# Padding the tiles that alpha, q and k are loaded into from 384 to 512 bytes per head

## The chip, the cores and the metric

The kernel runs on one core of one Trainium2 chip. The metric is the device time of one execution in microseconds (us). It is taken without the profiler; a further execution with the hardware profiler gives the profile. The engines are named as the profile names them: PE is TensorE (PEld its weight loads), DVE is VectorE, ACT is ScalarE, POOL is GpSimd and SP is SyncE, which here only issues transfers. DMA stands for the 16 engines that move data between DRAM and the on-chip memory SBUF.

## The reference

The first half is a recurrent linear attention with a decay for each key dimension; the second is a feed-forward layer whose hidden value is the largest of three products and zero.

```python
# q, k, v, alpha: (B, H, S, D) = (4, 8, 768, 48), float32; alpha in 0.8..1.0
for t in range(S):
    state = alpha[:, :, t, :, None] * state + np.einsum('bhd,bhe->bhde', k[:, :, t], v[:, :, t])
    y[:, :, t] = np.einsum('bhd,bhde->bhe', q[:, :, t], state)
x = y.transpose(0, 2, 1, 3).reshape(B * S, H * D)                 # 3072 x 384
h = np.maximum(np.maximum(x @ w1, x @ w2), x @ w3)                # w: 384 x 768
out = h @ w_out                                                   # 3072 x 384, float32
```

The feed-forward has no explicit rectifier in the reference. The kernel writes the largest of three as x @ w1 plus the larger of 0, x @ (w2 - w1) and x @ (w3 - w1); this is why it has a bypass product, w1 @ w_out, and differences of weights.

## The kernel before, in words

The sequence of 768 steps of each of the 4 batch entries is cut into 3 chunks of 256 steps, so there are 12 groups, numbered n = 4 * chunk + batch entry, and the four batch entries take turns. Within a group the 256 steps lie on 128 partitions, two neighbouring steps (r = 0, 1) on one partition. For each group there are four loads (`load`, L274), one each for alpha, q, k and v. A load brings, for each of 128 partitions and 8 heads, the two steps' 2 x 48 floats, which lie next to each other in DRAM: 384 bytes. For the first group each load is cut in two by heads, 4 heads each (HH). The destination tiles are in `ld`, named an, qn, kn and vn in the profile; each of them has NL = 5 buffers, so loads run up to five groups ahead of their use.

From alpha come the products of the two steps (`aa`, L351, on POOL or DVE), the logarithms (`la`, L356 and L361, on ACT), and by a matmul with a triangular matrix (L426) their sums along the chunk. The exponentials of these sums (ep and en, L435, on ACT) scale q and k (`qk`, L440, on POOL or DVE, 48 instructions in all, each for 4 heads). v is scaled and cast to half precision (L259 on ACT or L261 on POOL). Then come transposes (L465), the copy of the transposed q and k (L479), the scores within the chunk (L491), their masking (L499), the state (L523, L412, L400), and the output within the chunk (L578) and from the state (L556). The result is turned (L599) to xT, which the feed-forward reads.

The feed-forward of a group (`ffn`) is 36 products with the differences of weights (L622), their rectification and maximum (L631, L633, L638), the products with w_out and the bypass (L658, L655), a copy out of PSUM (L255) and a store of 192 KB (L674). It follows the attention of its group by about four groups. The weights come in four transfers from POOL's queue (`weights`, L288 and L291), 576 KB each as written; their differences are taken on DVE (L308).

All of this is cut into 821 steps, numbered as the code creates them. The order in which they are issued, and the engine and the PSUM banks of each, are written out by hand in the string `ORDER` (L26 to L70): `12A` is step 12 on ACT, `67G` step 67 on POOL. `Plan.emit` (L101) only checks that what a step reads has been issued before it. Each engine goes through its own instructions in that order and waits on semaphores for the others. All loads and stores are issued by SP in one queue; the weights are issued on POOL's queue among POOL's own work.

The tiles come from one pool and lie one behind the other in each partition, in the order in which they are created: constants first, then the 20 load tiles of `ld` (5 of alpha, 5 of q, 5 of k, 5 of v), and then all others.

Of the kernel before, what the change touches and what calls it, by code (L numbers as in the profile page):

```python
# [10 lines left out]
FP32 = mybir.dt.float32  # L11
# [103 lines left out]
def kernel(  # L115
# [14 lines left out]
    B, H, S, D = q.shape  # L130
# [3 lines left out]
    P = 128  # L134
# [43 lines left out]
    def homes(n, shape, dtype, name):  # L178
        return [sb.tile(shape, dtype, name=f"{name}{i}") for i in range(n)]

    NL, NQ, NT_, HH = 5, 6, 4, H // 2
    ld = {x: homes(NL, [P, H, 2, D], FP32, x + "n") for x in "aqkv"}
    aas = homes(2, [P, H, D], FP32, "aa")
    las = homes(3, [P, 2, H, DP], FP16, "la")
    eps = homes(3, [P, HH, 2, D], FP32, "ep")
# [545 lines left out]
```

## Time and profile before

| | us |
|---|---|
| median of 3 runs | 151.62 |
| lowest and highest run | 150.16, 151.63 |
| span of the profiled execution | 148.5 |
| PE busy in the span | 130.6 |
| DVE busy in the span | 121.9 |
| ACT busy in the span | 80.7 |
| POOL busy in the span | 71.8 |

The profiled execution's own time is its span, from the first instruction to the last; the times of the runs hold besides it what lies before and after. The page lists, for each group of instructions, its line and engine, what it writes and reads with partitions x elements and type, how many there are, their busy time, the mean duration in ns, and the idle time of the engine just before them with what ended it. The row of digits for DMA gives the busy share of the 16 DMA engines in 40 slices of 3.7 us each, in tenths. The chain is the work that ended last, followed backwards from the last instruction through what released each step.

The transfers of the page, by queue: q1 holds SP's loads and stores (53,584 packets, 23.60 MB, 63.4% of the 16 engines' time), q0 the weights that POOL issues (832 packets, 2.36 MB, 8.1%). DRAM was read at 23.63 MB and written at 4.72 MB.

### The profile page before, as it was taken

What the parts mean: (1) busy time and instruction counts of PE and PEld (TensorE: products, weight loads), DVE (VectorE), ACT (ScalarE), POOL (GpSimd) and SP (SyncE); (2) the same over time, 40 slices, a digit from 0 to 9 for tenths busy, and PEclk for the clock granted to TensorE, in tenths of its full rate; (3) what the DMA queues carried; (4) which work ended last, traced back from release to release, by engine and by line L of the source; (5) the groups of instructions that cost most, each with busy time, mean ns of one, the idle gap of its engine ahead of it and who ended that gap; (6) DMA issues with size and microseconds to landing.
All of it is one profiled execution on the core that took longest, in us unless ns stands there. A gap on an engine that the chain in (4) does not pass through costs nothing.

```text
span 148.5 us, 5617 instructions
## 1 busy us (share of the span) xinstructions
PE 130.6 (88%) x2389; PEld 101.7 (68%) x2389; DVE 121.9 (82%) x231; ACT 80.7 (54%) x182; POOL 71.8 (48%) x114
## 2 busy tenths in 40 slices
PE   0136588889999999999999999999999999999990
PEld 0025576767776678887687889777777788787670
DVE  6489996999899979998896899699698786789720
ACT  3665156796895987947877759328622820000011
POOL 8105810431859888999976678994720100000000
PEclk9999999999999999999999999999999999999999
DMA  4999999999999999999997299601211100031223
GB/s 111 257 261 262 258 214 212 279 231 265 270 262 265 261 275 267 262 288 268 233 279 188 79 246 280 200 3 60 106 57 57 53 4 0 4 119 40 85 99 134
DMA packets 54728, 26.34 MB, mean 177 GB/s; under 512 B 50736, under 2 KB 54320, under 8 KB 54704
## 3 DMA queue, kind: packets, MB, share of 16 engines
q1 hardware_dynamic: 53584, 23.60, 63.4%
q0 software_dynamic: 832, 2.36, 8.1%
q8 instruction: 18, 0.29, 0.9%
q10 hardware_dynamic: 288, 0.04, 0.3%
q14 instruction: 6, 0.05, 0.1%
HBM read 23.63 MB, written 4.72 MB: 191 GB/s over the span
## 4 chain that ended last, share of the span: by engine, by line
PE 65%; DMA 10%; POOL 6%; ACT 5%; DVE 4%; SPq 4%; issue 3%; POOLq 0%; DVEq 0%
PE psum L622 26%; PE psum L658 15%; PE psum L655 8%; DMA wcat<-in_moe_w_dram 6%; SPq L274 4%; DMA qn<-in_q_dram 4%; POOL qk L440 3%; PE psum L491 3%; PE psum L578 3%; PE psum L465 2%; PE psum L599 2%; PE psum L334 2%; PE psum L556 2%; PE psum L523 2%; POOL Z L400 1%
## 5 line engine op out<-in xcount | busy, mean ns | idle before, releaser
L622 PE MATMUL psum<-xT,d 128*128 128x256 f16 x432 | 54.1, 273 | 0.9 <-DVE d L308 0.5
L622 PEld LDWEIGHTS <-d 128*128 128x128 f16 x432 | 40.0, 98 | 7.0 <-DVE d L308 1.5
L499 DVE TENSOR_TENSOR LA<-psum,d 128x1024 f16<-128x1024 f32 x24 | 28.7, 1218 | 3.7 <-PE psum L491 2.8
L658 PE MATMUL psum<-wo,hT 128*128 128x384 f16 (+1 forms) x150 | 27.5, 320 | 0.0
L638 DVE TENSOR_TENSOR hT<-psum,hT 128x512 f16<-128x512 f32 x36 | 23.7, 681 | 2.9 <-PE psum L622 2.6
L440 POOL TENSOR_TENSOR qk<-qn,ep 128x384 f16<-128x384 f32 x18 | 18.3, 1026 | 11.3 <-DMA qn<-in_q_dram 9.2
L631 ACT ACTIVATE hT<-psum 128x512 f16<-128x512 f32 x28 | 16.4, 601 | 12.7 <-PE psum L622 12.3
L255 ACT COPY ob<-psum 128x384 f32<-128x384 f32 x14 | 6.7, 481 | 27.8 <-PE psum L658 27.8
L658 PEld LDWEIGHTS <-hT 128*128 128x128 f16 x150 | 14.5, 98 | 8.9
L440 POOL TENSOR_TENSOR qk<-kn,en 128x384 f16<-128x384 f32 x16 | 15.9, 999 | 9.0 <-ACT en L435 8.5
L479 DVE COPY qkT<-psum 128x1024 f16<-128x1024 f16 x24 | 16.0, 683 | 0.9 <-PE psum L465 0.7
L655 PE MATMUL psum<-past,xT 128*128 128x384 f16 (+1 forms) x75 | 15.8, 320 | 0.0
L259 ACT ACTIVATE xb<-psum,c 128x384 f16<-128x384 f32 x17 | 9.3, 583 | 9.0 <-PE psum L578 9.0
L435 ACT ACTIVATE en<-psum 128x384 f32<-128x384 f32 x24 | 11.5, 493 | 2.1 <-DVE psum L430 2.1
L465 PE MATMUL psum<-d,qk 64*128 64x64 f16 x384 | 8.8, 198 | 4.1 <-POOL qk L440 2.1
L435 ACT ACTIVATE ep<-psum 128x384 f32<-128x384 f32 x24 | 11.6, 493 | 1.1 <-DVE psum L430 0.8
L351 POOL TENSOR_TENSOR aa<-an 128x384 f32<-128x384 f32 x9 | 9.0, 1001 | 4.7 <-DVE qkT L479 4.2
L255 ACT CAST xT<-psum 128x384 f16<-128x384 f32 x20 | 9.4, 482 | 3.0 <-PE psum L599 2.8
L426 PE MATMUL psum<-la,c 128*128 128x192 f16 x24 | 6.1, 271 | 5.5 <-ACT la L361 5.5
L465 PEld LDWEIGHTS <-qk 64*128 64x128 f16 x384 | 7.0, 99 | 5.5 <-DVE qk L440 2.9
L400 POOL TENSOR_TENSOR Z<-U,G 48x192 f16<-48x192 f32 x10 | 5.0, 504 | 11.8 <-DVE U L412 11.5
L430 DVE TENSOR_TENSOR psum<-psum,la 128x192 f32<-128x192 f32 x24 | 8.5, 358 | 2.6 <-PE psum L426 1.8
(58 smaller groups left out, 196.4 us busy)
## 6 DMA issues: line engine op xcount, KB each, us to landing
out_dram<-ob SPq DMA_DIRECT2D x23, 192.0 KB, 2.0
an<-in_alpha_dram SPq DMA_DIRECT2D x11, 384.0 KB, 6.2
qn<-in_q_dram SPq DMA_DIRECT2D x11, 384.0 KB, 5.7
kn<-in_k_dram SPq DMA_DIRECT2D x11, 384.0 KB, 6.2
vn<-in_v_dram SPq DMA_DIRECT2D x11, 384.0 KB, 6.3
wcat<-in_moe_w_dram POOLq DMA_DIRECT2D x2, 576.0 KB, 10.3
w1s<-in_moe_w_dram POOLq DMA_DIRECT2D x1, 576.0 KB, 7.9
wo<-in_moe_w_out_dram POOLq DMA_DIRECT2D x1, 576.0 KB, 7.8
```

The costliest lines, as they stand in the source:

```text
L255: (nc.scalar.copy if eng == "ACT" else nc.vector.tensor_copy)(out=out, in_=in_)
L259: nc.scalar.activation(out=out, in_=in_, func=AFT.Copy, scale=factor)
L435: lambda eng, t=t, sign=sign: nc.scalar.activation(out=t, in_=live[Lk], func=AFT.Exp, scale=sign),
L440: lambda eng, w=w, x=x, e=e: on[eng].tensor_mul(qk[:, w, :, :, :D].rearrange("p r h d -> p h r d"), ld[x][n % NL][:, hs], e),
L465: nc.tensor.transpose(live["tp", v][:, i, at:at + HALF], qks[v % NQ][rows, w, r, 2 * j:2 * j + 2, :], ident[rows, rows])
L479: lambda eng: nc.vector.tensor_copy(out=qkT.rearrange("p i w j t -> p i (w j t)"), in_=live["tp", u]),
L499: lambda eng: nc.vector.tensor_mul(LA.rearrange("p a j r t -> p (a j) (r t)"), live[Ak].rearrange("p a (j t) -> p (a j) t", j=2), maskA.un ...
L622: nc.tensor.matmul(live[gk][:, jj, :], hidden(apart[g][j][:, kt], jj), xT[:, kt, :], start=(kt == 0), stop=(kt == NFT - 1))
L631: nc.scalar.activation(out=h, in_=live[gk], func=AFT.Relu)
L638: lambda eng, h=h, gk=gk: nc.vector.tensor_max(h, live[gk], h),
L655: nc.tensor.matmul(live[ok], xT[:, kt, i * P:(i + 1) * P], past[:, kt, cols], start=(kt == 0), stop=False)
L658: nc.tensor.matmul(live[ok], hT[:, kt, i * P:(i + 1) * P], wo16[:, kt, cols], start=False, stop=(kt == NJ - 1))
```

## The change

The tiles of alpha, q and k are created with 8 x 128 floats on each partition instead of 8 x 2 x 48. Of each head's 128 floats (512 bytes) the first 96 (384 bytes) are used, seen as 2 x 48 as before; the other 32 are neither written nor read. v's tiles keep 8 x 2 x 48 floats, back to back. All other code takes its views from these, so the loads write, and the engines read, the same elements at other places. Fifteen tiles grow from 3,072 to 4,096 bytes per partition.

```diff
     NL, NQ, NT_, HH = 5, 6, 4, H // 2
-    ld = {x: homes(NL, [P, H, 2, D], FP32, x + "n") for x in "aqkv"}
+    ld = {x: [t[:, :, :2 * D].rearrange("p h (r d) -> p h r d", r=2) for t in homes(NL, [P, H, 2 * D if x == "v" else P], FP32, x + "n")] for x in "aqkv"}
     aas = homes(2, [P, H, D], FP32, "aa")
```

## The prediction

> **What bounds the kernel now.** I read the page first: its busy shares, the rate of the transfers, and the costliest groups.
>
> ```profile
> span 148.5 us, 5617 instructions
> PE 130.6 (88%) x2389; PEld 101.7 (68%) x2389; DVE 121.9 (82%) x231; ACT 80.7 (54%) x182; POOL 71.8 (48%) x114
> DMA  4999999999999999999997299601211100031223
> DMA packets 54728, 26.34 MB, mean 177 GB/s; under 512 B 50736, under 2 KB 54320, under 8 KB 54704
> q1 hardware_dynamic: 53584, 23.60, 63.4%
> PE 65%; DMA 10%; POOL 6%; ACT 5%; DVE 4%; SPq 4%; issue 3%; POOLq 0%; DVEq 0%
> ```
>
> TensorE is the bound: it is busy for 88% of the span and holds 65% of the chain that ended last. The transfers are full for the first half of the span (the row of nines) and hold 10% of the chain. Nearly all packets are under 512 bytes: the 12 groups of four 384 KB loads make 12 x 4 x 1,024 = 49,152 packets of 384 bytes (one head, two rows of 48 floats). They are what the change touches.
>
> Next, the stages: columns are the stretch, its length, the busy time of PE, PEld, DVE, ACT and POOL, the granted clock, the share of the 16 DMA engines (over 1 when packets overlap) and the rate.
>
> ```profile
> core 0: us, PE busy (x) PEld busy (x) DVE busy (x) ACT busy (x) POOL busy (x), PEclk, DMA share, GB/s
> 0.00:5.00 5.00, 0.00 (x0) 0.10 (x1) 2.85 (x17) 1.60 (x2) 3.60 (x15) 1.00 0.59 134
> 5.00:10.00 5.00, 1.79 (x28) 0.90 (x27) 3.51 (x10) 4.33 (x13) 0.00 (x0) 1.00 1.20 272
> 10.00:15.00 5.00, 2.75 (x94) 2.14 (x88) 4.73 (x10) 2.14 (x5) 2.23 (x3) 1.00 1.27 263
> 15.00:20.00 5.00, 3.21 (x113) 2.78 (x117) 4.90 (x6) 0.95 (x2) 3.68 (x6) 1.00 1.19 244
> 20.00:25.00 5.00, 4.71 (x79) 3.88 (x79) 4.07 (x9) 3.17 (x9) 0.00 (x0) 1.00 1.06 215
> 25.00:30.00 5.00, 4.05 (x39) 3.23 (x38) 4.41 (x9) 3.80 (x9) 1.78 (x2) 1.00 1.14 261
> 30.00:35.00 5.00, 4.40 (x124) 3.44 (x123) 4.94 (x9) 4.76 (x10) 1.16 (x2) 1.00 1.15 254
> 35.00:40.00 5.00, 4.75 (x71) 3.52 (x68) 4.36 (x10) 3.26 (x8) 3.18 (x5) 1.00 1.04 256
> 45.00:50.00 5.00, 5.00 (x81) 3.21 (x80) 4.87 (x10) 3.33 (x10) 4.41 (x6) 1.00 1.22 264
> 75.00:80.00 5.00, 5.00 (x104) 3.77 (x103) 4.60 (x12) 4.01 (x11) 3.12 (x6) 1.00 1.05 284
> ```
>
> The reader is to see two regimes. Up to about 25 us TensorE is short of work; from 40 us it has no gap, so there a load may come earlier or later without moving the end, as long as it comes before its use. The granted clock is 1.00 throughout. The chain shows which transfers count in the first regime (start, length, what):
>
> ```profile
> 6.45 0.64 SPq L274
> 7.14 5.45 DMA qn<-in_q_dram
> 12.73 1.38 POOL qk L440
> 14.12 0.71 issue
> 14.83 0.80 POOL qk L440
> 15.77 9.15 DMA wcat<-in_moe_w_dram
> 25.42 0.56 DVE d L308
> 27.31 2.15 PE psum L622 x18
> ```
>
> The second group's q lands at 12.59 us, releases the multiply on POOL, and behind it on POOL's queue stand the weight loads, which land at 24.92 us and open the feed-forward part.
>
> **The change, part by part.** No instruction is added, removed or moved on any engine: the order is written out by hand and the dependencies are the same. Three things differ.
>
> *1. Where the loads write.* A load still writes 128 partitions x 8 heads x 384 bytes from the same addresses in DRAM, so 1,024 packets of 384 bytes. Before, the eight heads lay back to back (start every 384 bytes); now every 512, with a gap of 128. In the built program the first alpha tile starts at byte 17,856 of its partition in both kernels, which is 448 past a multiple of 512. Before, heads start at 448, 320, 192, 64 past such a multiple, in turn. Now all start at 448, since the new tiles are 4,096 bytes long. So 512 bytes per head do not bring alignment to 512: every head straddles such a boundary, where before three in four did. Counted in 256-byte blocks, a head touched 3 blocks (starts 448 and 192) or 2 (320 and 64), 2.5 in the mean; now always 3.
>
> What is a packet's time? At 263 to 284 GB/s over 16 engines, 16 x 384 bytes / rate gives 21.6 to 23.4 ns. All four starts are already in these rates, and nothing in the windows separates them. If the block count set the price, a, q and k would cost 20% more (3 against 2.5); if it plays no part, nothing. Below nothing: the best rate in the rows is 284 against 263 to 272 in the early stretch, so 4 to 8% could be won if the packing back to back were what holds the early packets up. I take nothing: the nearest rows are those of the loads themselves, in which every second head already starts as all will start now (192 past a 256-byte boundary). The ends +20% and -8% stay for the range.
>
> The Trainium skill ("DMA: Bandwidth & Descriptors", section "How a descriptor splits into AXI transactions") says that a descriptor is cut at 256-byte boundaries, and that one with an unaligned start also pays for the bytes before it. By that a write of 384 bytes starting 192 past a boundary is 18 beats and one starting 64 past it 14, so an estimate from that page is 16 in the mean before and 18 after, 12.5% more; the section's examples are reads, and no view of before shows what writes pay. This rule speaks against the change, and with it the slower rival below would cost +0.9 to +1.5 us in place of what is worked out there.
>
> *2. What the engines read.* Five kinds of instruction read the padded tiles. Alpha's readers (L351, L356) already step over half a head at a time: a step of 384 bytes becomes 512. The multiplies of L440 read one run of 384 floats before and four runs of 96 now.
>
> ```profile
> L440 POOL TENSOR_TENSOR qk<-kn,en 128x384 f16<-128x384 f32 x16 | 15.9, 999 | 9.0 <-ACT en L435 8.5 <-POOL Z L400 0.4
> L351 POOL TENSOR_TENSOR aa<-an 128x384 f32<-128x384 f32 x9 | 9.0, 1001 | 4.7 <-DVE qkT L479 4.2 <-DMA an<-in_alpha_dram 0.4
> 6.66 0.56 DVE L351 TENSOR_TENSOR aa<-an 128x384 f32<-128x384 f32 x1 [0.45 <-DMA an<-in_alpha_dram]
> 7.49 0.56 DVE L440 TENSOR_TENSOR qk<-kn,en 128x384 f16<-128x384 f32 x1
> L356 ACT ACTIVATE la<-an 128x384 f16<-128x384 f32 x11 | 5.9, 536 | 0.0
> L361 ACT ACTIVATE la<-aa 128x384 f16<-128x384 f32 x11 | 5.8, 526 | 1.0 <-POOL aa L351 0.8
> ```
>
> L351 reads both operands in runs of 48 with gaps, L440 one run; on POOL they take 1001 and 999 ns, on VectorE 0.56 and 0.56 us. On ScalarE, reading with gaps (L356) against without (L361) is 536 against 526 ns. So gaps cost at most 10 ns here. Upper bound: 10 ns x 48 multiplies = 0.5 us over two engines, little of it on the chain, where POOL has 6%. I take nothing.
>
> *3. Addresses and issue.* Fifteen tiles grow by 1,024 bytes, so what lies behind them moves by up to 15,360 bytes, a multiple of 512: their place in such blocks stays. The loads' issue on SP:
>
> ```profile
> 72.07 0.43 SPq L274 DMA_DIRECT2D qn<-in_q_dram  x1
> 75.83 0.38 SPq L274 DMA_DIRECT2D vn<-in_v_dram  x1
> L674 SPq DMA_DIRECT2D out_dram<-ob x25: 332/357/2130, 52.2 to 145.7; - x25
> ```
>
> An unblocked load of 1,024 packets is issued in 0.38 to 0.43 us, an output with 128 packets in 0.33 at least: the number of pieces hardly counts, and the early issues of about 1.4 us are the queue waiting for the engines. The form of the access (partition, head, 96 floats) is the same. Nothing again.
>
> Sum: 0. The span stays 148.5 us. The three runs' median, 151.62, stands 3.1 us above the span; that remainder lies outside what the profile shows, and I leave it. Forecast **151.6 us**. The runs shown spread from 150.16 to 151.63, about 1%, which is what a measurement of this kernel can tell from no change.
>
> **What a dearer or cheaper packet is worth.** Before q's second load lands at 12.59 us, SP has issued eight half loads and two whole ones: 8 x 192 + 2 x 384 KB = 2.36 MB, 8.9 us at 265 GB/s. Of these, v has 384 KB and a, q, k the other 83%. One per cent on their packets is 0.074 us there. Then the weights share the engines with queued loads:
>
> ```profile
> qn<-in_q_dram SPq DMA_DIRECT2D x11, 384.0 KB, 5.7
> wcat<-in_moe_w_dram POOLq DMA_DIRECT2D x2, 576.0 KB, 10.3
> ```
>
> From 12.6 to 25 us, 2.4 us x 263 + 5 x 244 + 5 x 215 GB/s = 2.9 MB go by; less two or three weight matrices of 0.59 MB, 1.2 to 1.75 MB are loads, 4.4 to 6.6 us at 265 GB/s: some 60% of 8.9 us again. After that the cover is the pace of the compute:
>
> ```profile
> L440 POOL TENSOR_TENSOR qk<-qn,ep x18: 992/1002/1379, 12.7 to 107.4; 128x384 f16<-128x384 f32 x18
> L440 DVE TENSOR_TENSOR qk<-qn,ep x6: 541/555/559, 8.9 to 88.8; 128x384 f16<-128x384 f32 x6
> ```
>
> The 24 multiplies of q run from 8.9 to 107.4 us: 4.3 us for each, 8.6 for a group, whose four loads are 1.57 MB or 5.9 us at 265 GB/s. The loads would have to be some 40% slower before they set the pace of the whole. If they did, the time would be far off, up in the 160s.
>
> **Rivals.** *Slower: each head's write pays for the third block.* Place: the loads before 25 us; price 20% on a, q, k. The first 8.9 us grow by 0.83 x 20% = 1.5 us, the weights come up to 0.9 us later still, so +1.5 to +2.4 and 153.1 to 154.0 us. TensorE's idle time between 25 and 40 us (0.95 + 0.60 + 0.25 = 1.8 us) may swallow some. It decides (over 1%) from about 15% more per packet. For it: the start of the span is bound by transfers and the change leaves only straddling starts. Against it: nothing in the rates shows two prices. A heavier form belongs here too: if the engine now joins the eight back-to-back writes of a partition into one run of 3,072 bytes, and the gaps stop it, the price could be higher than 20%. The packet count shows 384-byte pieces already, so I give it little. I name 153.4 us for this rival, and 0.30.
>
> *Faster: separate slots ease the early loads.* In the early stretch and at 45 us the packets overlap (share 1.20 to 1.27 at 263 to 272 GB/s), at 75 us they don't (1.05 at 284). If neighbouring heads in one 512-byte block hold each other up, the gap lets the early loads run at 284: 4 to 8% of 8.9 us, 0.4 to 0.6 us, and with the weights up to 0.9: 150.7 to 151.2. Over 1% it would need 15% faster packets, which no row shows. Against it: the same packing is there at 75 us, where the rate is full. I give 0.17 to a time over 1% below, mostly for what the rows can't show.
>
> *No effect, because the change doesn't reach what limits a packet*: it stays at 384 bytes, under 512 as before. This is the forecast, 150.2 to 152.6 by the runs' spread on either side, 0.53.
>
> **How the numbers follow.** 0.53 for the forecast, within 1% (150.1 to 153.1); 0.30 for slower by over 1%; 0.17 for faster. The range: 149.6 takes in the faster rival and 0.6 below it for an unshown gain, 154.4 the slower rival's upper end with as much again of the spread; below and above these I leave 0.08 and 0.12.
>
> **What would show it.** Right: q1's packets and share unchanged (53,584, 63.4%), 263 to 272 GB/s between 5 and 15 us, q's second load landing near 12.6 us, the weights near 25, L440 on POOL at 999 to 1026 ns. The slower rival: fewer GB/s before 15 us at the same packet count, and landings later by a tenth. The faster: over 280 GB/s there. Wrong in another way: L440 or L351 longer on POOL or VectorE, or a packet count that changes.

## The result and the profile after

The changed kernel takes 155.84 us in the median of its runs (155.64 to 157.21), the kernel before 150.89 us beside it. The ratio is 1.036, with a 95% interval of 1.029 to 1.042: the change costs 5 us. The forecast was no change, with a range up to 154.4; the slower rival gave 153.1 to 154.0 us. Each ratio, here and below, compares undisturbed runs with runs of the kernel before beside them on the same chip, while a median in us takes in all runs; so across chips the ratios are to be compared.

The page of the changed kernel, in the lines that answer to those shown of before:

```profile
span 154.0 us, 5617 instructions
PE 133.2 (86%) x2389; PEld 102.8 (67%) x2389; DVE 123.4 (80%) x231; ACT 81.1 (53%) x182; POOL 71.9 (47%) x114
q1 hardware_dynamic: 53584, 23.60, 71.4%
PE 36%; ACT 0%; issue 0%
```

The span is 5.5 us longer. The packets are the same in number and bytes, but their share of the engines' time is 71.4% of a longer span, where it was 63.4%: each packet is in flight longer. The chain can't be followed back beyond 95.7 us in this trace, so the stages have to show the rest (columns as in the prediction):

```profile
core 0: us, PE busy (x) PEld busy (x) DVE busy (x) ACT busy (x) POOL busy (x), PEclk, DMA share, GB/s
5.00:10.00 5.00, 1.33 (x12) 0.45 (x11) 3.15 (x8) 4.49 (x13) 0.00 (x0) 1.00 1.31 228
10.00:15.00 5.00, 3.25 (x104) 2.59 (x104) 4.17 (x11) 2.23 (x6) 0.97 (x1) 1.00 1.33 225
15.00:20.00 5.00, 2.31 (x76) 1.89 (x76) 4.93 (x6) 0.61 (x1) 3.91 (x7) 1.00 1.32 239
20.00:25.00 5.00, 4.34 (x98) 3.48 (x99) 4.79 (x10) 2.46 (x5) 1.00 (x1) 1.00 1.05 214
45.00:50.00 5.00, 5.00 (x107) 3.66 (x108) 4.56 (x11) 4.48 (x12) 3.34 (x6) 1.00 1.28 225
75.00:80.00 5.00, 4.77 (x66) 3.73 (x66) 4.28 (x9) 4.57 (x13) 4.10 (x5) 1.00 1.23 229
```

Wherever only loads run, 263 to 284 GB/s have become 225 to 229. Only from 15 to 25 us, where the weights run beside the loads, is the rate about as before (239 against 244, then 214 against 215). The instructions on POOL that read the padded tiles are no slower:

```profile
L351 POOL TENSOR_TENSOR aa<-an 128x384 f32<-128x384 f32 x9 | 9.0, 999 | 9.7 <-DVE LA L499 8.3 <-DMA an<-in_alpha_dram 1.2
L440 POOL TENSOR_TENSOR qk<-qn,ep 128x384 f16<-128x384 f32 x18 | 18.1, 1018 | 13.3 <-DMA qn<-in_q_dram 9.9 <-ACT ep L435 2.6 <-ACT xb L259 0.7
```

So what the change itself made dearer is the transfers. Two things that come of it show up only in single rows, and are taken up below: slower products on TensorE after 28 us, although the clock of the rows above is 1.00, and three longer instructions on VectorE near 90 us.

### The profile page after: what moved, and what is told of

Its sections match the earlier page's. It is cut to its first block, busy times and chain, and to the rows that moved or that the text cites. A ratio compares the mean times of both kernels' runs of the same rounds, so it can differ in the third digit from the quotient of the medians.

```text
span 154.0 us, 5617 instructions
## 1 busy us (share of the span) xinstructions
PE 133.2 (86%) x2389; PEld 102.8 (67%) x2389; DVE 123.4 (80%) x231; ACT 81.1 (53%) x182; POOL 71.9 (47%) x114
## 3 DMA queue, kind: packets, MB, share of 16 engines
q1 hardware_dynamic: 53584, 23.60, 71.4%
## 5 line engine op out<-in xcount | busy, mean ns | idle before, releaser
L622 PE MATMUL psum<-xT,d 128*128 128x256 f16 x432 | 55.7, 278 | 1.8 <-DVE d L308 1.8
L622 PEld LDWEIGHTS <-d 128*128 128x128 f16 x432 | 41.0, 100 | 8.4 <-DVE d L308 2.0
L499 DVE TENSOR_TENSOR LA<-psum,d 128x1024 f16<-128x1024 f32 x24 | 28.7, 1217 | 3.5 <-PE psum L491 2.6
L440 POOL TENSOR_TENSOR qk<-qn,ep 128x384 f16<-128x384 f32 x18 | 18.1, 1018 | 13.3 <-DMA qn<-in_q_dram 9.9
L440 POOL TENSOR_TENSOR qk<-kn,en 128x384 f16<-128x384 f32 x16 | 16.2, 1013 | 8.9 <-ACT en L435 7.8
L351 POOL TENSOR_TENSOR aa<-an 128x384 f32<-128x384 f32 x9 | 9.0, 999 | 9.7 <-DVE LA L499 8.3
L491 PE MATMUL psum<-qkT 48*64 48x128 f16 x384 | 9.7, 235 | 0.9 <-DVE qkT L479 0.5
L400 POOL TENSOR_TENSOR Z<-U,G 48x192 f16<-48x192 f32 x10 | 5.0, 502 | 11.6 <-DVE U L412 11.3
```

What stands on the lines that cost most here:

```text
L440: lambda eng, w=w, x=x, e=e: on[eng].tensor_mul(qk[:, w, :, :, :D].rearrange("p r h d -> p h r d"), ld[x][n % NL][:, hs], e),
L491: nc.tensor.matmul(live[Ak][i * HALF:(i + 1) * HALF, p, at:at + P], qkT[rows, i, 1, j, r * HALF:(r + 1) * HALF], qkT[rows, i, 0, j, :], st ...
L499: lambda eng: nc.vector.tensor_mul(LA.rearrange("p a j r t -> p (a j) (r t)"), live[Ak].rearrange("p a (j t) -> p (a j) t", j=2), maskA.un ...
L622: nc.tensor.matmul(live[gk][:, jj, :], hidden(apart[g][j][:, kt], jj), xT[:, kt, :], start=(kt == 0), stop=(kt == NFT - 1))
```

## Experiments: what makes a packet dearer

The question is which property of the new addresses the packets pay for. Four theories: the number of 256-byte blocks that a head's 384 bytes touch (before 3 and 2 in turn, 2.5; changed 3, and with v's unchanged 2.5 a mean of 2.875); the crossing of 512-byte boundaries (before three heads in four, changed every head); the gap between heads, so that writes are no longer back to back; or the distance of the start from the boundary below it. All are told apart by moving the load tiles by a few bytes, with unused bytes ahead of them and, to keep all later tiles at the same place within 512 bytes, the rest of 512 behind them.

**Slots of 512 bytes, starting at 0.**

```diff
+    sb.tile([P, 16], FP32, name="ahead")
     ld = {x: [t[:, :, :2 * D].rearrange(...) for t in homes(NL, [P, H, 2 * D if x == "v" else P], ...)] for x in "aqkv"}
+    sb.tile([P, 112], FP32, name="behind")
```

> The changed kernel with 64 unused bytes ahead of the load tiles, so that every head of alpha, q and k starts at 0 past a multiple of 512 (v, back to back, at 0 or 128 past a multiple of 256); all else keeps its place. If the number of 256-byte blocks that a write touches sets its price: 2 blocks for all, where before had 2.5 and the changed kernel 3: the early rate is at least the 264 to 272 GB/s of before and the time 149 to 151 us. If the crossing of 512-byte boundaries does: none is crossed, the same 149 to 151 us. If the gap between heads does (writes no longer back to back): no help, about 226 GB/s and 155.8 us.

Measured: 148.75 us, 0.987 of before (0.983 to 0.991).

**Heads back to back, starting at 0**: the kernel before with the same two lines.

> The kernel before with the same 64 bytes ahead: heads back to back, starting 0, 384, 256, 128 past a multiple of 512. Blocks of 256: 2 for all (before: 2 and 3 in turn), faster than before if writes bind there, 149 to 150.9 us, and a rate above 265 GB/s in the early stretch. Boundaries of 512: two of four cross (before: three of four), a little faster. Gap theory: no gap in either, 150.9 us.

Measured: 149.20 us, 0.991 of before (0.986 to 0.995).

**Slots of 512 bytes, starting at 256**: as the first, with 80 floats ahead and 48 behind.

> The changed kernel with the load tiles moved by 320 bytes: every head of alpha, q and k starts at 256 past a multiple of 512, so that it touches 2 blocks of 256 bytes but crosses a boundary of 512. Blocks of 256: as fast as with starts at 0, 149 to 151 us. Boundaries of 512: as slow as the changed kernel, 155.8 us. Gap theory: 155.8 us.

Measured: 149.53 us, 0.988 of before (0.983 to 0.992).

**Slots of 512 bytes, starting at 128**: 48 floats ahead, 80 behind.

> The changed kernel with the load tiles moved by 192 bytes: every head of alpha, q and k starts at 128 past a multiple of 512 and ends at the next, 2 blocks of 256 bytes, no boundary of 512 crossed. If the number of 256-byte blocks is the price: as with starts at 0, 149 to 151 us. If a write also pays for the bytes between the 256-byte boundary and its start (128 here, 192 in the changed kernel, 64 and 192 in turn before): as before, 150.9 us, and above the run with starts at 0 if that one is faster than before. Gap theory: 155.8 us.

Measured: 148.91 us, 0.988 of before (0.981 to 0.995).

**Slots of 512 bytes, starting at 160**: 56 floats ahead, 72 behind.

> The changed kernel with the load tiles moved by 224 bytes: every head of alpha, q and k starts at 160 past a 256-byte boundary, 32 bytes later than in the run at 128, so that its last 32 bytes fall into a third block; v at 160 and 32 in turn. If each block touched has a price, whatever lies in it: as the changed kernel, about 226 GB/s early and 155 to 156.5 us. If the price goes by bytes or by the distance from the boundary: close to the run at 128, below 151 us.

Measured: 156.50 us, 1.037 of before (1.026 to 1.047).

One window, 5 to 15 us, where the engines move loads and little else, gives the price of each arrangement; the last column is the rate. First before, then changed:

```profile
5.00:15.00 10.00, 4.55 (x116) 3.04 (x115) 8.24 (x19) 6.46 (x18) 2.23 (x3) 1.00 1.23 267
```

```profile
5.00:15.00 10.00, 4.58 (x116) 3.04 (x115) 7.32 (x18) 6.71 (x18) 0.97 (x1) 1.00 1.32 227
```

Slots of 512 bytes starting at 0, then heads back to back from 0:

```profile
5.00:15.00 10.00, 5.27 (x132) 3.44 (x131) 8.64 (x19) 7.18 (x19) 3.52 (x6) 1.00 1.12 306
```

```profile
5.00:15.00 10.00, 5.25 (x132) 3.44 (x131) 8.27 (x18) 6.76 (x18) 3.53 (x5) 1.00 1.13 309
```

Slots starting at 256, at 128 and at 160:

```profile
5.00:15.00 10.00, 4.81 (x128) 3.23 (x129) 8.14 (x18) 6.45 (x18) 3.03 (x4) 1.00 1.12 293
```

```profile
5.00:15.00 10.00, 4.49 (x116) 2.92 (x115) 8.38 (x18) 6.82 (x18) 3.16 (x4) 1.00 1.12 305
```

```profile
5.00:15.00 10.00, 4.10 (x108) 2.81 (x107) 6.69 (x16) 6.71 (x18) 0.29 (x1) 1.00 1.31 227
```

| heads of alpha, q, k | blocks of 256, mean of the four tensors | GB/s, 5 to 15 us | ns for a packet on one engine (16 x 384 bytes / rate) | ratio to before |
|---|---|---|---|---|
| slots, at 0 | 2 | 306 | 20.1 | 0.987 |
| back to back, from 0 | 2 | 309 | 19.9 | 0.991 |
| slots, at 256 | 2 | 293 | 21.0 | 0.988 |
| slots, at 128 | 2 | 305 | 20.1 | 0.988 |
| back to back, from 448 (before) | 2.5 | 267 | 23.0 | 1 |
| slots, at 448 (changed) | 2.875 | 227 | 27.1 | 1.036 |
| slots, at 160 | 2.875 | 227 | 27.1 | 1.037 |

The block count orders all seven, at 9.2 to 10.5 ns per block. (At 256 the first weights begin within the window and lower its rate; up to 14 us it is 298.) The gap counts for nothing: slots and back-to-back heads are alike at 2 blocks. Boundaries of 512 count for nothing: a head from 256 on crosses one and is as cheap. The distance from the boundary counts for nothing: a start at 128 costs what one at 0 does. And 32 bytes more, from 128 to 160, put the last 32 bytes into a third block and cost 4.9 points of the time of before. Blocks of 64 or 128 bytes are out as well: before and changed, every start is 64 past a multiple of 128, so the counts would be 6 and 4 in both. So is the number of 256-byte blocks that are written only in part: it is two for every head of alpha, q and k, before and changed. v, which lies behind and moves along, is in the means (2.5 at 448 and at 160, else 2).

The Trainium skill ("DMA: Bandwidth & Descriptors", section "How a descriptor splits into AXI transactions") cuts a descriptor at 256-byte boundaries; these runs agree with the cut, for writes. Its charge for the bytes between the boundary and an unaligned start they don't show: an estimate by it is 16 beats for a start at 128 and 12 for one at 0, and the rates are 305 and 306 GB/s.

## Experiments: where five microseconds come from

By block count a, q and k cost 20% more, as the slower rival had it, and yet the time went up by 5 us, where it gave 1.5 to 2.4. The next kernels give a price to part of the groups only. Slots are 512 bytes; alpha, q and k of some groups start at 192 (3 blocks), those of the others at 128 (2 blocks); v stays at 2.5 in all groups, where the runs at 2 blocks above have 2 for v too.

```diff
-    ld = {x: homes(NL, [P, H, 2, D], FP32, x + "n") for x in "aqkv"}
+    sb.tile([P, 48], FP32, name="ahead")
+    room = {x: homes(NL, [P, H * P], FP32, x + "n") for x in "aqk"}
+
+    def heads(x, n):
+        t, off = room[x][n % NL], 16 if n in (0, 1, 2,) else 0
+        return t.rearrange("p (h w) -> p h w", h=H)[:, :, off:off + 2 * D].rearrange("p h (r d) -> p h r d", r=2)
+
+    ld = {x: [heads(x, n) for n in range(NG)] for x in "aqk"}
+    sb.tile([P, 16], FP32, name="between")
+    vs = homes(NL, [P, H, 2, D], FP32, "vn")
+    ld["v"] = [vs[n % NL] for n in range(NG)]
+    sb.tile([P, 64], FP32, name="behind")
...
-            t = ld[x][n % NL]
+            t = ld[x][n]
...
```

The other places that read `ld` change in the same way.

**Groups 0 to 2 at 3 blocks:**

> Slots of 512 bytes as in the changed kernel; alpha, q and k of groups 0 to 2 are written at 192 past a 256-byte boundary (3 blocks, as in the changed kernel), those of groups 3 to 11 at 128 (2 blocks); v as before (2.5). With all groups at 2 blocks 148.9 to 149.5 us are to be expected, with all at 3 about 155.8. If only the wait for the first loads is paid for: all of it, 155 to 156 us. If the delay builds up as the traces show it (2.6 us at the first q, 3.5 at the weights, 5.5 at 40 us, 6.7 at the end, against the run with starts at 0): the first two parts, 152.5 to 153.5 us.

Measured: 154.52 us, 1.023 of before (1.013 to 1.033).

**Groups 3 to 11 at 3 blocks** (the list in `heads` is 3 to 11):

> The other way round: groups 0 to 2 at 2 blocks, groups 3 to 11 at 3. If only the first loads are paid for: 149 to 149.5 us. If the delay builds up: the parts after the weights, 151.5 to 152.5 us.

Measured: 152.62 us, 1.009 of before (1.005 to 1.013).

**Groups 6 to 11 at 3 blocks:**

> Groups 0 to 5 at 2 blocks, groups 6 to 11 (loads from about 45 us on) at 3. If loads are covered by the pace of the compute once TensorE has no gap: 149 to 149.5 us, although the rate falls to about 226 GB/s there. If the late step of the changed kernel's delay (1.2 us near 90 us) comes from late loads: 150 to 151 us.

Measured: 150.55 us, 0.997 of before (0.991 to 1.003), not told apart from before nor, by the intervals, from 0.988 with all at 2 blocks.

From all at 2 blocks (0.988) to all at 3 (1.036) are 4.8 points. The first three groups alone cost 3.5 of them (four runs), the other nine alone 2.1. That this is more than 4.8 together is not clear of the intervals, of about one point each, and v's third blocks are counted in both. Each half of the load stream has its price. Neither one-sided expectation held: "only the first loads" gave 155 to 156 and 149 to 149.5, and for the first three groups the build-up's 152.5 to 153.5 was too low as well (its 151.5 to 152.5 for the others was missed by 0.1).

How the delay builds up is read from the same instruction in each trace. The masking of the scores (LA, L499; L510 in the experiments) for the pair near 46 us and the last pair, in the timelines of VectorE, first before:

```profile
46.46 2.36 DVE L499 TENSOR_TENSOR LA<-psum,d 128x1024 f16<-128x1024 f32 x2
...
119.51 2.36 DVE L499 TENSOR_TENSOR LA<-psum,d 128x1024 f16<-128x1024 f32 x2 [0.54 <-PE psum L491]
```

Changed:

```profile
50.70 2.36 DVE L499 TENSOR_TENSOR LA<-psum,d 128x1024 f16<-128x1024 f32 x2
...
124.97 2.35 DVE L499 TENSOR_TENSOR LA<-psum,d 128x1024 f16<-128x1024 f32 x2 [0.54 <-PE psum L491]
```

Groups 0 to 2 at 3 blocks, then groups 3 to 11:

```profile
50.46 2.36 DVE L510 TENSOR_TENSOR LA<-psum,d 128x1024 f16<-128x1024 f32 x2
...
123.50 2.36 DVE L510 TENSOR_TENSOR LA<-psum,d 128x1024 f16<-128x1024 f32 x2 [0.54 <-PE psum L502]
```

```profile
44.96 2.36 DVE L510 TENSOR_TENSOR LA<-psum,d 128x1024 f16<-128x1024 f32 x2
...
122.64 2.36 DVE L510 TENSOR_TENSOR LA<-psum,d 128x1024 f16<-128x1024 f32 x2 [0.54 <-PE psum L502]
```

The changed kernel is 4.2 us late near 46 us and 5.5 at the end. With dear loads in the first three groups alone it is 4.0 late at both places: nearly all of the early part, none of the late one. With dear loads from group 3 on it is 1.5 us early at 46 us, by its cheap start, and 3.1 late at the end.

The early part, piece by piece, in POOL's and VectorE's timelines of the changed kernel:

```profile
14.03 1.36 POOL L440 TENSOR_TENSOR qk<-qn,ep 128x384 f16<-128x384 f32 x1 [9.76 <-DMA qn<-in_q_dram]
...
37.16 0.99 POOL L351 TENSOR_TENSOR aa<-an 128x384 f32<-128x384 f32 x1 [8.31 <-DVE LA L499]
38.13 0.19 POOL L383 TENSOR_TENSOR G<-e 128x4 f32<-128x4 f32 x1
```

```profile
27.62 0.89 DVE L308 TENSOR_TENSOR d<-wcat,w1s 128x768 f16<-128x768 f16 x1 [2.10 <-DMA wcat<-in_moe_w_dram]
...
38.35 0.74 DVE L400 TENSOR_TENSOR Z<-psum,G 48x192 f16<-48x192 f32 x2 [1.24 <-POOL G L383]
```

The second group's q is 1.3 us late (12.73 before), the weights' difference 2.2 us (25.42 before). Then comes a wait that the prediction doesn't name. Group 3's alpha load is issued at 19.84 us and its product (L351) starts on POOL at 37.16. Before, the same product started at 31.83:

```profile
31.83 0.99 POOL L351 TENSOR_TENSOR aa<-an 128x384 f32<-128x384 f32 x1 [4.22 <-DVE qkT L479]
```

Both rows name VectorE as the releaser, which is not so: the product reads only alpha; before, it ran ahead of the masking (LA, at 32.35) that the changed kernel's row names, and in the changed kernel the copy that the row of before names (qkT) is over at 35.89. What it waits for is its load. Before, the load is issued at 17.78 us and takes 13.9 us to land, at 31.7; in the changed kernel it takes 17.2 and lands at 19.84 + 17.2 = 37.0. In the run with groups 0 to 2 at 3 blocks the row says so itself:

```profile
36.93 0.99 POOL L362 TENSOR_TENSOR aa<-an 128x384 f32<-128x384 f32 x1 [8.16 <-DMA an<-in_alpha_dram]
```

There group 3's own alpha is written at 2 blocks; it is late because it stands behind the dear loads and shares the engines with the weights. What it shares is seen before the change, in the queues between 17 and 22 us:

```profile
q0 software_dynamic: 222, 0.95, 94.1%
q1 hardware_dynamic: 442, 0.16, 16.0%
```

The weights take 94% of the engines' time there and the loads 16%. Behind the product on POOL stands G (L383), for G waits Z on VectorE (1.24 us, L400), and in VectorE's queue all else waits. Before, G ended at 32.98 us and Z began at 33.60, so there were 0.6 us to spare: the product is 5.3 us late, Z 4.7 (38.35). A wait of 0.57 us that the kernel before has at 38.37 is then gone, and 4.2 us of delay are left. This is how 5.3 us of one load became 2 us more of delay between 25 and 46 us.

On the way there TensorE was slower too. In the changed kernel it stands still for 1.75 us until the weights' difference is there, and then:

```profile
28.56 4.44 PE L622 MATMUL psum<-xT,d 128*128 128x256 f16 x24 [1.75 <-DVE d L308]
```

That is 24 products in 4.44 us, where before 18 took 2.15; up to 32 us the median of one is 421 ns, before 273. The clock of the rows is 1.00 there, but the trace holds no clock record ahead of 31.96 us (before: 25.54), so this 1.00, and that of every earlier row in both kernels, says nothing on the clock. The run with groups 0 to 2 at 3 blocks has records there, products of 421 ns too, and a lower clock:

```profile
30.00:35.00 5.00, 5.00 (x63) 3.82 (x61) 3.52 (x9) 3.34 (x7) 0.00 (x0) 0.69 1.19 247
```

So TensorE's clock was lower for some microseconds behind the longer wait; why is not shown. VectorE is 3.5 us late by then (34.60 against 31.07), but by these rows it cost nothing in the end, since Z had to wait for group 3's alpha all the same. No run tests that apart.

The late part is the 1.2 us between 46 us and the end (4.24 us late there, 5.46 here). It is absent when groups 3 to 11 are cheap. VectorE's timeline shows where it arises, first before, then changed:

```profile
83.23 1.21 DVE L499 TENSOR_TENSOR LA<-psum,d 128x1024 f16<-128x1024 f32 x1
84.36 0.70 DVE L351 TENSOR_TENSOR aa<-an 128x384 f32<-128x384 f32 x1
84.99 0.55 DVE L440 TENSOR_TENSOR qk<-kn,en 128x384 f16<-128x384 f32 x1
85.46 0.68 DVE L638 TENSOR_TENSOR hT<-psum,hT 128x512 f16<-128x512 f32 x1
86.06 0.61 DVE L400 TENSOR_TENSOR Z<-U,G 48x192 f16<-48x192 f32 x1
```

```profile
87.55 1.21 DVE L499 TENSOR_TENSOR LA<-psum,d 128x1024 f16<-128x1024 f32 x1
88.68 0.70 DVE L351 TENSOR_TENSOR aa<-an 128x384 f32<-128x384 f32 x1
89.36 0.87 DVE L440 TENSOR_TENSOR qk<-kn,en 128x384 f16<-128x384 f32 x1
90.16 0.68 DVE L638 TENSOR_TENSOR hT<-psum,hT 128x512 f16<-128x512 f32 x1
90.76 1.11 DVE L400 TENSOR_TENSOR Z<-U,G 48x192 f16<-48x192 f32 x1
```

Up to 83 us the delay has hardly grown (4.3 us). Then there is no wait: VectorE has no gap, and three of its instructions take longer, 0.87 and 1.11 us in place of 0.55 and 0.61, and an L440 on q 1.05 (at 94.01) in place of 0.55 (at 88.83), 1.3 us together. The run at 160 has the same three at 0.89, 1.10 and 1.04 us; with groups 0 to 2 alone at 3 blocks they take 0.55, 0.61 and 0.55. L400 reads no padded tile, and with groups 0 to 2 alone dear L440 reads padded ones too, so the padding as such isn't it. POOL works beside them; what makes them longer is not shown.

With the loads dear from group 3 on, TensorE has gaps again after 40 us (columns as above), and VectorE is at work nearly all of that time:

```profile
50.00:55.00 5.00, 3.96 (x61) 2.73 (x61) 4.94 (x7) 3.69 (x10) 3.36 (x6) 1.00 1.26 235
```

```profile
50.10 1.80 DVE L394 TENSOR_TENSOR G<-e 128x4 f32<-128x4 f32 x1
```

Before, this G takes 0.38 us, and the two instructions ahead of it 0.15 and 0.35 in place of 0.91 and 1.12. These three make 2.9 of the 4.6 us that this kernel, in its profiled and slowest run, loses between 46 us and the end, before some of it is caught up. POOL waits for single loads beside them (0.79 us for k at 46.00). So what late loads cost after 40 us passes in good part through longer instructions on VectorE, which the loads reach only by shifting what runs at the same time; that link is argued, not shown.

**The rest of the tiles.** Last, whether the weights' and output tiles, which also lie 192 past a 256-byte boundary, want the same: 64 bytes ahead of the load tiles and none behind moves all of them to multiples of 256.

```diff
+    sb.tile([P, 16], FP32, name="ahead")
     ld = {x: homes(NL, [P, H, 2, D], FP32, x + "n") for x in "aqkv"}
```

> The kernel before with 64 unused bytes ahead of the load tiles and nothing behind them, so that every later tile moves by 64 bytes as well: the loads at 2 blocks for every head, and also the weights' and the output tiles (192 past a 256-byte boundary before) at a multiple of 256. If starts matter for the loads alone: as with heads back to back from 0, 149 to 149.5 us. If they matter for the weights (18 in place of 19 blocks in 4,608 bytes) or for what the stores read, up to 0.5 us less, the weights landing earlier by up to 5%.

Measured: 149.75 us, 0.992 of before (0.987 to 0.997). The run beside it, with the loads alone at 0:

> The kernel with heads back to back from 0 once more, for comparison on the same chip: 0.99 of the kernel before.

Measured: 148.94 us, 0.990 of before (0.986 to 0.994). No gain from the other tiles, and the weights land no sooner (all moved, then loads alone):

```profile
wcat<-in_moe_w_dram POOLq DMA_DIRECT2D x2, 576.0 KB, 10.4
```

```profile
wcat<-in_moe_w_dram POOLq DMA_DIRECT2D x2, 576.0 KB, 10.0
```

Any of the arrangements at 2 blocks beats both kernels; heads back to back with 64 unused bytes ahead are the smallest edit, one line, and need no larger tiles.

## Why the prediction was wrong

*Part 1, where the loads write: this step failed.* The facts were right: starts at 448, 3 blocks where there were 2.5, no alignment to 512. The value taken was not. "Nothing" was chosen because all four starts were "already in these rates" and nothing separated them. But a rate over starts that take turns is a mean; it can't show that they are equal. The end that was kept, +20% on a, q and k, is the one that holds: 15% over the four tensors by blocks, 18% measured (27.1 against 23.0 ns a packet). That term, put at nothing, is what the forecast lacked. The gain that the same thinking would have shown, 64 bytes of shift, was not seen at all.

*What a dearer packet is worth: too small by half.* The first two terms held: q 1.3 us late (1.5 predicted), the weights 2.2 (2.4 predicted at the upper end). The sum stopped there, at 25 us, with TensorE's gaps from 25 to 40 us as a cushion. They were the opposite, a time in which the compute still waited for loads; the stage that transfers set lasts until group 3's alpha lands, 31.7 us before and 37.0 us after, and adds 2 us. "The granted clock is 1.00 throughout" was read from rows that hold no record ahead of 25.54 us; TensorE's products after 28 us show a lower one.

*The cover after 40 us held in the changed kernel up to 83 us, but its size was overrated.* VectorE is 4.2 us late near 46 us and 4.3 at 83. The last 1.2 us come from longer instructions on VectorE near 90 us, for which the prediction has no term. "Some 40% slower before they set the pace" was worked out from whole groups' means, and is too much: loads from group 3 on, dear as in the changed kernel (18% above before, 35% above the arrangements at 2 blocks), cost 2.1 points against 2 blocks. A mean over 8.6 us per group hides that POOL waits for single loads, and that shifted work on POOL and VectorE can cost time without any wait.

*Parts 2 and 3 were right, as far as the padding goes.* L351 takes 999 ns on POOL (1001 before), L440 on q 1018 (1026); the packet counts are the same to the last one.

*The rivals.* The slower one had the mechanism, its first place and its price; its time was short by 1.8 to 2.7 us for the reasons above, and its rise, reckoned from 151.62 where the runs beside the changed kernel gave 150.89, by 2.6 to 3.5. Of its heavier form, joined writes that the gap would split, nothing is seen: slots and back-to-back heads cost the same. The faster rival, neighbours in one 512-byte block that hold each other up, is out for the same reason.

## What to carry to other kernels

When a transfer writes many small pieces, count for the built addresses how many 256-byte blocks each piece touches, from the tile's real start: a pitch of a power of two aligns nothing if the base isn't aligned, and here a shift of 64 bytes without padding was worth 1% while padding without the shift cost 3.6%. A rate that is a mean over two kinds of pieces says nothing on their difference. And when a transfer gets dearer, follow it to the last load that the compute has to wait for, with everything queued ahead of it, not to the first stage that looks covered.

## What was not expected of the hardware

The price of a write of 384 bytes goes in steps with the blocks of 256 bytes that it touches, 9.2 to 10.5 ns each on one engine, whatever part of a block is written: from a start at 128 to one at 160, 32 bytes in a third block took the rate from 305 to 227 GB/s. At 2 blocks the loads ran at 293 to 309 GB/s, above the 263 to 284 of the windows shown of before. Aligning the output and the weights' tiles, whose pieces are 1,536 and 4,608 bytes, showed no gain.

Instructions on VectorE took far longer in some runs with nothing in their own operands changed: one of 128 x 4 elements 1.80 us in place of 0.38. And a clock of 1.00 in a row of the profile stood for a stretch without a record: products took 421 ns there and 273 later.
